# Letting five down-projection blocks be promised at once, with four written, in a kernel that plans its own TensorE order

## The chip, the core and the metric

The kernel runs on one core of one Trainium2 chip. The metric is the device time in microseconds (us) from launch to end, the median of several runs. A profile of one execution goes with it; its span, from the first to the last instruction, is a little shorter than the device time.

## The reference, cut to what matters

Two attention steps with 32 learned queries, then a gated feed-forward layer on each of the 4 x 12416 rows of 128 channels. Nearly all the work is in the last four lines.

```python
def mab(q, kv):                                  # attention without projections
    s = scale * (q @ kv.transpose(0, 2, 1)); s = s - s.max(-1, keepdims=True)
    a = np.exp(s); a /= a.sum(-1, keepdims=True) + 1e-09
    return a @ kv
h = mab(I, x)                                    # 32 rows per batch, from all of x
x = mab(x, h).reshape(B * S, D)                  # 49664 x 128
rms = np.sqrt(np.mean(x * x, axis=-1, keepdims=True) + 1e-06)
xn = x / rms * rms_g
g = xn @ w_gate; silu = g * (1.0 / (1.0 + np.exp(-g)))   # 128 -> 1536
val = xn @ w_val                                         # 128 -> 1536
return (silu * val @ w_out).astype(np.float32)           # 1536 -> 128
```

## The kernel before

The feed-forward part is cut into 100 *units* of up to 512 rows (25 per batch: 20 of 512 rows, 4 of 480, 1 of 256), and each unit into 12 *slots*, one per block of 128 hidden channels: 1200 slots. A slot makes a gate product and a value product on TensorE (PE), silu on ScalarE (ACT), and their product `t` on VectorE (DVE):

```python
def slot(j, products, steps, tanh):
    products(0)
    g = bank()
    nc.tensor.matmul(g[:, 0:T], sg[:, ts(j, P)], a[:, 0:T], start=True, stop=True)         # L682
    sl = silp.tile([P, 512], F32, name="silu")
    ...
        nc.scalar.activation(sl[:, 0:T], g[:, 0:T], AF.Silu)                               # L690
    products(1)
    v = bank()
    nc.tensor.matmul(v[:, 0:T], sv[:, ts(j, P)], a[:, 0:T], start=True, stop=True)         # L693
    t = v if kinds.get((b, u, j)) == "sums" else up.tile([P, 512], F32, name="u")
    ...
        nc.vector.tensor_tensor(out=t[:, 0:T], in0=sl[:, 0:T], in1=v[:, 0:T], op=ALU.mult) # L699
    steps()
    if (b, u, j) in kinds:
        soon(1, lambda: three(j, t))
    else:
        plain.append(lambda: project(wo[:, j, :], t[:, 0:T]))                              # L618, f32
```

Each block `t` then has to go through the down projection, `t` times 128 rows of `w_out`, added up in PSUM over the unit's 12 blocks. There are two ways. A *plain* block is one float32 product (`acc<-u,wo`). A *split* block is written as two float32r factors and a difference of them, and takes three float32r products (`u<-xn,xn`, a second one into `u`, `acc<-xn,more`) with weights that were split in the same manner. Splitting costs work on other engines; it has two forms, *sums* and *differences*:

```python
def three(j, t):
    assert kws.get("out", 0) < RING
    ...                                            # hi, lo, d: one of RING = 4 sets of buffers, in turn
    if kind == "sums":
        nc.scalar.activation(hi, v, AF.Copy, scale=(1.0 - 2.0 ** -13) * 2.0 ** -12)        # L664 ACT
        nc.vector.scalar_tensor_tensor(out=lo, in0=hi.bitcast(F32), scalar=-4096.0, in1=v, # L665 DVE
                                       op0=ALU.mult, op1=ALU.add)
    else:
        nc.scalar.activation(d, v, AF.Copy, scale=1.0 - 2.0 ** -13)                        # L668 ACT
        nc.gpsimd.tensor_tensor(out=lo, in0=v, in1=d.bitcast(F32), op=ALU.subtract)        # L669 POOL
    def rest():
        if kind != "sums":
            nc.scalar.activation(hi, d.bitcast(F32), AF.Copy, scale=2.0 ** -12)            # L673 ACT
        nc.gpsimd.tensor_tensor(out=d, in0=hi.bitcast(F32), in1=lo.bitcast(F32), op=ALU.subtract)  # L674 POOL
        kara.append(lambda: project3(j, hi, lo, d))
    soon(1, rest)

def project3(j, hi, lo, d):
    ...
    nc.tensor.matmul(ups[:, 0:T], weight_of(0, j), hi, start=st["k"] == nk, stop=False)    # L638
    nc.tensor.matmul(ups[:, 0:T], weight_of(1, j), lo, start=False, stop=not st["k"])      # L640
    if not st["k"]:                                # the unit's last split block
        o = st["o"] = outp.tile([P, 512], F32, name="o")
        nc.scalar.activation(o[:, 0:T], ups[:, 0:T], AF.Copy, scale=1.0 + 2.0 ** -12)      # L643 ACT
    project(weight_of(2, j), d)                                                            # L618
    kws["out"] -= 1
```

`soon(1, ...)` runs a step at the end of the next slot: a block whose `t` belongs to slot n is written to a set of ring buffers in slot n+1 (`three`), finished in slot n+2 (`rest`), and its products come later. A unit that has split blocks also needs one addition more at its end, on DVE (L626).

Which blocks are split, and when each product is issued, is decided before any instruction is recorded, by a *rehearsal*. It walks through the slots with a clock for each engine, fed with costs written in the kernel, and keeps the result in `kinds` (which blocks, which form) and `picks` (which products go ahead of the gate product and of the value product in each slot). Its parts that matter here:

```python
MADE = {"sums": ((-.16,), (0, .6, .49), (0, 0, 0, 1.25)), "differences": ((-.16,), (0, 0, .53, 1.25), (0, 0, .52, 1.25))}
LIMIT = (0, 0.8, 0.8, 2.6)

def fits(k, kind, behind):         # would any engine fall too far behind PE in the next 8 slots?
    ...
    before = list(ahead())
    load(k, *MADE[kind])
    if all(x <= max(most, y + 0.1) for now, old in zip(ahead(), before) for x, y, most in zip(now, old, LIMIT)):
        return True
    load(k, *MADE[kind], sign=-1)

def decide(b, k, u, j):
    n = b * NU * NJ + k
    if (j >= NK or b == 0 and (u < 2 or k < 26) or (b, u) == flat[-1] and j > 6 or split["out"] > RING - 1 or
            near(b, k, -3, 2)):
        return None                # a plain block
    ...
    return next((kind for kind in ("sums", "differences") if fits(n, kind, behind)), None)
```

In each slot of the rehearsal, `choose` issues products that are ready while more than about `RESERVE` blocks are queued, `fill` issues more where PE would wait for a PSUM bank, and a loop issues plain blocks whose `u` buffer is needed again (9 of them, `LAG + 4`). `RESERVE` is 6. Elsewhere in the slots stand the steps of the attention for the next batch and the normalisation ("seam") steps, among them one slow power operation on GpSimd (POOL, L521).

Of the kernel before, what the change touches and what calls it, by code (L numbers as in the profile page):

```python
# [17 lines left out]

P = 128
R = 4  # L20
LAG = 5


@with_exitstack
def kernel(
# [72 lines left out]
    NU = len(units)  # L98

    NK = NJ - 2  # L100
    RING, RESERVE = 4, 6

    def pool(name, bufs, **kw):
        return ctx.enter_context(tc.tile_pool(name=name, bufs=bufs, **kw))
# [8 lines left out]
    once = pool("once", 1)  # L113
    halves = pool("halves", 1)
    astk = pool("astk", 2)
    silp = pool("silp", 3)
    up = pool("up", LAG + 4)
    outp = pool("outp", 2)
    ps_gv = pool("ps_gv", 5, space=PSUM)
    ps_acc = pool("ps_acc", 2, space=PSUM)  # L120
# [77 lines left out]
    if wide:  # L198
        t = scp.tile([P, SCW], F32, name="sc")
# [365 lines left out]
    plain, kara, waiting = [], [], []  # L565
# [175 lines left out]
    one = weight[1, 0]  # L741
# [39 lines left out]
    turn_a, square, turn_z, scale, root, apply, turn_b, split = seam(0, 0)  # L781
# [39 lines left out]
    def load(k, *costs, sign=1):  # L821
        for i, one in enumerate(costs):
            for e, us in enumerate(one):
                loads[k + i][e] += sign * us
# [72 lines left out]
    for k, (b, s) in enumerate(order):  # L897
# [5 lines left out]
        for late_by, one in enumerate(following):  # L903
            for i, step in enumerate(seam(*one)):
                j = ((14, 17, 18, 21, 22, 23, 29, 31) if k else (32, 33, 34, 35, 36, 36, 39, 41))[i]
                n, j = divmod(j, NJ)
# [4 lines left out]
    flat = [(b, u) for b in range(B) for u in range(NU)]  # L911
# [11 lines left out]
    def near(b, k, first, last):  # L923
        return any(e + first <= k < e + last for e in plans[b][1])

    def given(b, k, u, j):
        return plans[b][0].get(k, []) + seams.get((b, u, j), [])

    LIMIT = (0, 0.8, 0.8, 2.6)
    kinds, picks = {}, {}  # L930

    def rehearse():

        at = dict.fromkeys(ENGINES, 0.0)
        free, open_banks = [0.0] * 5, {}
        queues, uses, later, left = {"plain": [], "three": []}, [0], [], {}
        split = {"out": 0, "u3": 0.0, "all": 0}

        def run(e, us, *after):
            at[e] = max([at[e]] + [one + 0.04 for one in after]) + us  # L940
            return at[e] + TAIL[e]

        def bank():
            return free.index(min(free))

        def soon(k, step):
            later.append([k, step])
# [7 lines left out]
        def issue(kind, to):  # L955
            to.append(kind)
            t, unit, w = queues[kind].pop(0)[:3]
            split["all"] -= 1
            st = left[unit]
            if kind == "plain":  # L960
                end = run("PE", 0.858 * w, t)
            else:
                if st["three"] == 0:
                    run("PE", 0, split["u3"])
                end = run("PE", 0.697 * w, t)
                split["out"] -= 1
                st["three"] += 1
                st["open"] -= 1
            st["left"] -= 1
            st["end"] = end  # L970
            if not st["left"] and st["all"]:
                close(unit, w)

        def close(unit, w):
            st = left[unit]
            if st["three"]:
                split["u3"] = run("ACT", 0.47 * w, st["end"])

            def finish():
                run("DVE", 0.6 * w, st["end"], split["u3"])  # L980
                soon(1, lambda: run("DVE", 0.63 * w))

            soon(1, finish)

        def choose(to, most):
            done = 0
            while done < most:
                now = at["PE"] + 0.05
                if has("three", now):
                    issue("three", to)  # L990
                elif has("plain", now):
                    issue("plain", to)
                else:
                    break
                done += 1
            return done

        def fill(to, until):
            while until > at["PE"] + 0.25:
                now = at["PE"] + 0.05  # L1000
                kind = next((kind for kind in ("three", "plain") if has(kind, now)), None)
                if kind is None:
                    break
                issue(kind, to)
# [20 lines left out]
        def fits(k, kind, behind):  # L1025

            def ahead():
                now = list(behind)
                for i in range(k, k + 8):
                    now = [max(0.0, x + one - loads[i][0]) for x, one in zip(now, loads[i])]  # L1030
                    yield list(now)

            before = list(ahead())
            load(k, *MADE[kind])
            if all(x <= max(most, y + 0.1) for now, old in zip(ahead(), before) for x, y, most in zip(now, old, LIMIT)):
                return True
            load(k, *MADE[kind], sign=-1)

        def decide(b, k, u, j):
            n = b * NU * NJ + k  # L1040
            if (j >= NK or b == 0 and (u < 2 or k < 26) or (b, u) == flat[-1] and j > 6 or split["out"] > RING - 1 or
                    near(b, k, -3, 2)):
                return None
            s = at["PE"]
            behind = [0.0] + [max(0.0, at[e] - s - off) for e, off in (("DVE", 1.2), ("ACT", 0.45), ("POOL", 1.45))]
            return next((kind for kind in ("sums", "differences") if fits(n, kind, behind)), None)

        def slot(b, k, u, j, tanh):
            w = per2[units[u][0]] * m / 512.0
            st = left.setdefault((b, u), dict(left=NJ, three=0, open=0, all=False, slots=0, end=0.0))  # L1050
            kind = decide(b, k, u, j)
            first, second = picks[b, k] = [], []
            gi = bank()
            fill(first, free[gi])
            g = run("PE", 0.2325 * w, free[gi])
            silu = run("ACT", 0.5 * w, g)
            if tanh:
                silu = run("DVE", 0.6 * w, silu)
            free[gi] = silu
            least = 1 if near(b, k, 0, 4) or (b, u) == flat[-1] else RESERVE + 2 * near(b, k, -2, 0)  # L1060
            choose(second, min(2, max(0, split["all"] - least + 1)))
            if kind != "sums":
                uses[0] += 1
                while queues["plain"] and queues["plain"][0][3] <= uses[0] - (LAG + 4):
                    issue("plain", second)
            vi = bank()
            fill(second, free[vi])
            v = run("PE", 0.2325 * w, free[vi])
            t = run("DVE", 0.6 * w, v, silu)
            free[vi] = 1e9 if kind == "sums" else t  # L1070
            for one in later:
                one[0] -= 1
            while any(not one[0] for one in later):
                one = next(one for one in later if not one[0])
                later.remove(one)
                one[1]()
            names = [step.__name__ for step, _ in given(b, k, u, j)]
            for name in names:
                if name in ("exp1_of", "exp2") and k in plans[b][1]:
                    run("ACT", 1.28)  # L1080
                do(name)
            if near(b, k, 2, 3):
                run("ACT", 1.28)
            if kind:
                kinds[b, u, j] = kind
                split["out"] += 1
                st["open"] += 1

                def three():
                    hi = run("ACT", (0.49 if kind == "sums" else 0.53) * w, t)  # L1090
                    if kind == "sums":
                        lo = free[vi] = run("DVE", 0.6 * w, hi)
                    else:
                        lo = run("POOL", 1.25 * w, hi)

                    def rest():
                        h = hi if kind == "sums" else run("ACT", 0.52 * w, hi)
                        d = run("POOL", 1.25 * w, lo, h)
                        queues["three"].append((d + 0.05, (b, u), w))

                    soon(1, rest)

                soon(1, three)
            else:
                queues["plain"].append((t + 0.05, (b, u), w, uses[0]))
            split["all"] += 1
            st["slots"] += 1
            if st["slots"] == NJ:
                st["all"] = True
                if not st["left"]:  # L1110
                    close((b, u), w)

        for b in range(B):
            for k, (u, j) in slots(b):
                slot(b, k, u, j, (b, k) in by_tanh)
        return at

    rehearsed = rehearse()

    for b in range(B):  # L1120
# [59 lines left out]
```

## Time and profile before

| | |
|---|---|
| device time, median of 3 runs | 1646.5 us (1646.23 to 1646.5) |
| span of the profiled execution | 1644.2 us |
| TensorE (PE) busy | 1620.6 us, 99% |
| VectorE (DVE) busy | 1431.0 us, 87% |
| ScalarE (ACT) busy | 1156.8 us, 70% |
| GpSimd (POOL) busy | 1007.2 us, 61% |
| granted TensorE clock | 0.999 |
| split blocks | 603 of 1200 |

How to read it: a matmul's recorded duration overlaps that of the next one, so the distance between the starts of two neighbours tells what one costs PE, and not its duration. The same holds, less strongly, for DVE, ACT and POOL, whose records also overlap a little when one instruction follows another directly. In the groups, "out<-in" names the tiles; a float32 matmul has two records, a float32r matmul has one. The ring buffers of the split blocks carry the name `xn`, the split weights `xn` or `more`.

### The profile page before, as it was taken

The numbers are of one execution on the slowest core, as the hardware profiler recorded it, in microseconds if no ns is written. First come the engines' busy times: TensorE is split into PE (matmuls) and PEld (weight loads), VectorE is DVE, ScalarE is ACT, GpSimd is POOL, SyncE is SP. The second block draws the span as 40 slices with busy tenths as digits, with TensorE's granted clock in tenths as the row PEclk, the third lists the DMA queues.
The fourth block names the chain that finished last, engine by engine and source line by source line (L and its number), as shares of the span: only waits on it lengthen the run. The fifth ranks groups of instructions, "written<-read, shape, count | busy, mean of one in ns | idle before, by whom it ended". The sixth has DMA issues, their size and how long they took to land.

```text
span 1644.2 us, 24663 instructions
## 1 busy us (share of the span) xinstructions
PE 1620.6 (99%) x6983; PEld 1070.2 (65%) x6983; DVE 1431.0 (87%) x2469; ACT 1156.8 (70%) x2104; POOL 1007.2 (61%) x804
## 2 busy tenths in 40 slices
PE   8899999999999999999999999999999999999998
PEld 6545666656676666665667666666567676666676
DVE  4878987899899998889889999789989999999997
ACT  4566777767776777676777676766677777777775
POOL 1246763766467755476567575466747767767764
PEclk9999999999999999999999999999999999999999
DMA  6455434443453241624435324253221112212221
GB/s 259 90 71 84 82 65 84 102 95 59 68 87 60 42 90 29 135 70 84 70 58 82 60 39 88 55 124 74 49 38 35 32 31 39 39 28 38 39 37 25
DMA packets 389176, 112.47 MB, mean 68 GB/s; under 512 B 365072, under 2 KB 369712, under 8 KB 386480
## 3 DMA queue, kind: packets, MB, share of 16 engines
q1 hardware_dynamic: 388304, 110.82, 34.3%
q8 instruction: 55, 0.90, 0.2%
q14 instruction: 81, 0.66, 0.1%
q10 hardware_dynamic: 736, 0.08, 0.0%
HBM read 53.95 MB, written 27.00 MB: 49 GB/s over the span
## 4 chain that ended last, share of the span: by engine, by line
PE 89%; DVE 2%; ACT 2%; issue 1%; POOL 1%; SPq 1%; DMA 1%; DVEq 0%; POOLq 0%; ACTq 0%
PE acc L618 35%; PE gv L682 17%; PE gv L693 15%; PE u L640 8%; PE u L638 8%; PE gv L327 3%; PE gv L504 1%; PE gv L383 1%; ACT sc L444 1%; POOL rs L521 0%; DVE u L699 0%; SPq L147 0%; PE gv L458 0%; DVE xn L665 0%; ACT silu L690 0%
## 5 line engine op out<-in xcount | busy, mean ns | idle before, releaser
L674 POOL TENSOR_TENSOR xn<-xn,xn 128x512 fp32r<-128x512 f32 (+2 forms) x603 | 750.1, 1255 | 451.1 <-DVE xn L665 271.4
L690 ACT ACTIVATE silu<-gv 128x512 f32<-128x512 f32 (+2 forms) x1186 | 689.7, 586 | 375.6 <-PE gv L682 351.5
L693 PE MATMUL gv<-a,sv 128*128 128x512 f32 (+2 forms) x1188 | 680.2, 573 | 0.5 <-ACT silu L690 0.2
L618 PE MATMUL acc<-u,wo 128*128 128x512 f32 (+2 forms) x1194 | 591.6, 580 | 0.0
L682 PE MATMUL gv<-a,sg 128*128 128x512 f32 (+2 forms) x1188 | 486.2, 409 | 3.9 <-ACT silu L690 2.4
L699 DVE TENSOR_TENSOR u<-silu,gv 128x512 f32<-128x512 f32 (+2 forms) x650 | 423.3, 659 | 59.0 <-PE gv L693 41.7
L699 DVE TENSOR_TENSOR gv<-silu,gv 128x512 f32<-128x512 f32 (+2 forms) x536 | 359.8, 673 | 86.8 <-PE gv L693 66.7
L665 DVE SCALAR_TENSOR_TENSOR xn<-xn,gv 128x512 fp32r<-128x512 f32 (+2 forms) x537 | 354.4, 660 | 9.8 <-ACT xn L664 5.5
L682 PEld LDWEIGHTS gv<-a,sg 128*128 128x128 f32 x1188 | 224.5, 189 | 207.4 <-ACT silu L690 45.0
L664 ACT ACTIVATE xn<-gv 128x512 fp32r<-128x512 f32 (+2 forms) x537 | 314.6, 586 | 52.2 <-DVE gv L699 44.1
L693 PEld LDWEIGHTS gv<-a,sv 128*128 128x128 f32 x1188 | 224.4, 189 | 157.4 <-issue 77.1
L618 PEld LDWEIGHTS acc<-u,wo 128*128 128x128 f32 x1194 | 224.0, 189 | 55.3 <-issue 12.0
L618 PE MATMUL acc<-xn,more 128*128 128x512 f32 (+2 forms) x603 | 235.1, 390 | 2.6 <-POOL xn L674 2.6
L638 PE MATMUL u<-xn,xn 128*128 128x512 f32 (+2 forms) x603 | 233.2, 387 | 0.0
L640 PE MATMUL u<-xn,xn 128*128 128x512 f32 (+2 forms) x356 | 137.7, 387 | 0.0
L618 PEld LDWEIGHTS acc<-xn,more 128*128 128x128 f32 x603 | 113.3, 188 | 29.9 <-POOL xn L674 6.3
L638 PEld LDWEIGHTS u<-xn,xn 128*128 128x128 f32 x603 | 113.4, 188 | 24.1 <-issue 4.2
L521 POOL TENSOR_TENSOR rs<-ms,mhalf 128x16 f32<-128x16 f32 (+2 forms) x28 | 75.9, 2710 | 68.8 <-DVE ms L516 68.0
L669 POOL TENSOR_TENSOR xn<-u,xn 128x512 fp32r<-128x512 f32 (+1 forms) x66 | 85.1, 1289 | 19.3 <-ACT xn L668 19.1
L640 PE MATMUL u<-xn,more 128*128 128x512 f32 (+2 forms) x247 | 95.9, 388 | 0.0
L640 PEld LDWEIGHTS u<-xn,xn 128*128 128x128 f32 x356 | 66.9, 188 | 15.2 <-issue 0.2
L629 DVE STREAM_TRANSPOSE o<-o 128x512 f32<-128x512 f32 (+2 forms) x92 | 63.0, 685 | 0.0
(151 smaller groups left out, 1009.1 us busy)
## 6 DMA issues: line engine op xcount, KB each, us to landing
out_dram<-o SPq DMA_DIRECT2D x320, 64.0 KB, 2.0
xT<-in_x_dram SPq DMA_DIRECT2D x60, 256.0 KB, 4.7
xn<-in_x_dram SPq DMA_DIRECT2D x60, 256.0 KB, 5.1
a<-hi SPq DMA_DIRECT2D x156, 64.0 KB, 2.0
a<-lo SPq DMA_DIRECT2D x156, 64.0 KB, 2.0
xn<-in_x_dram SPq DMA_DIRECT2D x5, 1024.0 KB, 9.9
xn<-w SPq DMA_DIRECT2D x18, 256.0 KB, 3.2
out_dram<-o SPq DMA_DIRECT2D x64, 60.0 KB, 2.0
```

The source lines that it names most:

```text
L521: nc.gpsimd.tensor_tensor(out=rs, in0=st["ms"], in1=mhalf[rows, 0:n], op=ALU.pow)
L618: nc.tensor.matmul(acc[:, 0:T], lhsT, rhs, start=st["left"] == NJ, stop=st["left"] == 1)
L638: nc.tensor.matmul(ups[:, 0:T], weight_of(0, j), hi, start=st["k"] == nk, stop=False)
L640: nc.tensor.matmul(ups[:, 0:T], weight_of(1, j), lo, start=False, stop=not st["k"])
L664: nc.scalar.activation(hi, v, AF.Copy, scale=(1.0 - 2.0 ** -13) * 2.0 ** -12)
L665: nc.vector.scalar_tensor_tensor(out=lo, in0=hi.bitcast(F32), scalar=-4096.0, in1=v, op0=ALU.mult, op1=ALU.add)
L669: nc.gpsimd.tensor_tensor(out=lo, in0=v, in1=d.bitcast(F32), op=ALU.subtract)
L674: nc.gpsimd.tensor_tensor(out=d, in0=hi.bitcast(F32), in1=lo.bitcast(F32), op=ALU.subtract)
L682: nc.tensor.matmul(g[:, 0:T], sg[:, ts(j, P)], a[:, 0:T], start=True, stop=True)
L690: nc.scalar.activation(sl[:, 0:T], g[:, 0:T], AF.Silu)
L693: nc.tensor.matmul(v[:, 0:T], sv[:, ts(j, P)], a[:, 0:T], start=True, stop=True)
L699: nc.vector.tensor_tensor(out=t[:, 0:T], in0=sl[:, 0:T], in1=v[:, 0:T], op=ALU.mult)
```

## The change

It changes the rehearsal alone; buffers, arithmetic and the engines' instructions for one block stay as they are. It is meant to let more blocks take the three-product way, and to keep TensorE from meeting a factor that isn't ready.

- Ring sets are now counted from when `three` writes them (`split["made"]`) and not from when the block is decided. A block may be decided while four others are outstanding (`> RING` in place of `> RING - 1`), so five are decided at most and four written. Where all four sets are written and a further `three` is due in this slot, one split block is issued first.
- `RESERVE` goes from 6 to 7: one more block stays outstanding before `choose` issues any.
- `fits` lets an engine's backlog that is already over its limit grow by 0.25 us, where it was 0.1.
- silu in the rehearsal waits for its buffer (three of them). `LAG` is gone; `HELD` is the same nine `u` buffers as before.

```diff
-    RING, RESERVE = 4, 6
+    RING, RESERVE, HELD, SILU = 4, 7, 9, 3
...
-    silp = pool("silp", 3)
-    up = pool("up", LAG + 4)
+    silp = pool("silp", SILU)
+    up = pool("up", HELD)
...
+        taken = [0.0] * SILU
-        split = {"out": 0, "u3": 0.0, "all": 0}
+        split = {"out": 0, "u3": 0.0, "all": 0, "made": 0}
...
                 split["out"] -= 1
+                split["made"] -= 1
...
-            if all(x <= max(most, y + 0.1) for now, old in zip(ahead(), before) for x, y, most in zip(now, old, LIMIT)):
+            if all(x <= max(most, y + 0.25) for now, old in zip(ahead(), before) for x, y, most in zip(now, old, LIMIT)):
...
-            if (j >= NK or b == 0 and (u < 2 or k < 26) or (b, u) == flat[-1] and j > 6 or split["out"] > RING - 1 or
+            if (j >= NK or b == 0 and (u < 2 or k < 26) or (b, u) == flat[-1] and j > 6 or split["out"] > RING or
...
-            silu = run("ACT", 0.5 * w, g)
+            silu = run("ACT", 0.5 * w, g, taken[-SILU])
...
-                while queues["plain"] and queues["plain"][0][3] <= uses[0] - (LAG + 4):
+                while queues["plain"] and queues["plain"][0][3] <= uses[0] - HELD:
                     issue("plain", second)
+            while split["made"] == RING and any(one[0] == 1 and one[1].__name__ == "three" for one in later):
+                issue("three", second)
...
             t = run("DVE", 0.6 * w, v, silu)
+            taken.append(t)
...
                 def three():
+                    split["made"] += 1
```

More of the change, by code (lines that the diff above doesn't have):

```diff
@@ L20 @@
 R = 4
-LAG = 5
 @with_exitstack
```

## The prediction

> **What bounds the kernel now.** I read the first page from the top: busy shares, slices, groups. TensorE stands at 99% in every slice, at full clock.
>
> ```profile
> PE 1620.6 (99%) x6983; PEld 1070.2 (65%) x6983; DVE 1431.0 (87%) x2469; ACT 1156.8 (70%) x2104; POOL 1007.2 (61%) x804
> PE   8899999999999999999999999999999999999998
> PEclk9999999999999999999999999999999999999999
> ```
>
> A busy share of 99% proves little, since the records of matmuls overlap. So the second view is TensorE's timeline, where only the starts are read. First a stretch with split blocks, then one with plain blocks alone.
>
> ```profile
> 600.76 0.40 PE L682 MATMUL gv<-a,sg 128*128 128x512 f32 x1
> 600.99 0.39 PE L638 MATMUL u<-xn,xn 128*128 128x512 f32 x1
> 601.23 0.40 PE L640 MATMUL u<-xn,more 128*128 128x512 f32 x1
> 601.46 0.40 PE L618 MATMUL acc<-xn,more 128*128 128x512 f32 x1
> 601.69 0.40 PE L693 MATMUL gv<-a,sv 128*128 128x512 f32 x1
> ```
>
> ```profile
> 250.79 0.40 PE L682 MATMUL gv<-a,sg 128*128 128x512 f32 x1
> 251.02 1.88 PE L618 MATMUL acc<-u,wo 128*128 128x512 f32 x4
> 252.34 0.80 PE L693 MATMUL gv<-a,sv 128*128 128x512 f32 x1
> 252.98 0.40 PE L682 MATMUL gv<-a,sg 128*128 128x512 f32 x1
> ```
>
> Starts are 0.233 us apart, so a gate or value product costs 0.233 and a split block three of them, 601.69 - 600.99 = 0.70 us. From 250.79 to 252.98 there is one gate, one value and two plain blocks (four records): 2.19 - 2 x 0.233 = 1.72, or 0.86 us for a plain block. A split block saves TensorE 0.16 us at 512 columns.
>
> Third, is there slack in TensorE's stream? Adding these costs over the whole timeline from 100 us on, with about 1.0 us for the four matmuls of a score step and 0.87 for a normalisation square, leaves some 26 us unexplained in 1540. So the stream is closed to under 2%, and the end is the sum of TensorE's work. The open gaps are few. The largest kind by far in the last batch is this one, in the timeline of all engines:
>
> ```profile
> 1355.45 2.90 POOL L521 TENSOR_TENSOR rs<-ms,mhalf 128x16 f32<-128x16 f32 x1 [1.25 <-DVE ms L516]
> ...
> 1358.32 1.28 POOL L674 TENSOR_TENSOR xn<-xn,xn 128x512 fp32r<-128x512 f32 x1
> ...
> 1358.55 0.40 PE L640 MATMUL u<-xn,more 128*128 128x512 f32 x1
> ...
> 1359.65 0.50 PE L618 MATMUL acc<-xn,more 128*128 128x512 f32 x1 [0.71 <-POOL xn L674]
> ```
>
> The power operation holds GpSimd for 2.90 us, the factor d is finished late, and the third product of the block waits (0.71 us idle, about 0.87 by the starts). It recurs near 1420 and 1481, and with 0.45 us near 1542: 2.6 us in all.
>
> **What the Trainium skill says.** "Perfetto Trace Analysis", section "Identifying the Most-Contended Engine", says that matmul busy time misjudges the distance to the limit because matmuls are pipelined. This trace agrees: records of 0.39 to 0.40 us whose starts are 0.233 apart. "TensorE: Matmul & The Clock Gate", section "Back-to-back issue gap", gives N/2.4 + 2.5 ns for an isolated gap, 216 ns for 512 columns, and a shorter one for a sustained stream of bf16; the trace shows 233 ns here and I use that. "Perfetto Trace Analysis", section "Optimizing Scalar/DVE Operations", says that half of an instruction's access overhead overlaps with the next one; the trace agrees, as DVE records of 0.68 us follow each other at 0.60 us, so an 87% busy DVE is less full than it looks. "GPSIMD Engine Reference", section 3.1, gives about 2.6 cycles an element for a two-input tensor operation, an estimate of 1.11 us for 512 columns from that page at its 1.2 GHz; the trace has 1.29 us, and 1.24 between starts.
>
> **The change, part by part.** The instruction list of the built program shows what the new rehearsal decides. These are the rows of the page that its counts are held against:
>
> ```profile
> L674 POOL TENSOR_TENSOR xn<-xn,xn 128x512 fp32r<-128x512 f32 (+2 forms) x603 | 750.1, 1255 | 451.1 <-DVE xn L665 271.4
> L618 PE MATMUL acc<-u,wo 128*128 128x512 f32 (+2 forms) x1194 | 591.6, 580 | 0.0
> L665 DVE SCALAR_TENSOR_TENSOR xn<-xn,gv 128x512 fp32r<-128x512 f32 (+2 forms) x537 | 354.4, 660 | 9.8 <-ACT xn L664 5.5
> L669 POOL TENSOR_TENSOR xn<-u,xn 128x512 fp32r<-128x512 f32 (+1 forms) x66 | 85.1, 1289 | 19.3 <-ACT xn L668 19.1
> ```
>
> Before: 603 split blocks, 537 by sums and 66 by differences, and 597 plain ones (1194 records). After: 706 split, 568 by sums (+31) and 138 by differences (+72), and 494 plain. Of the 103 that change side, 79 have 512 columns, 17 have 480 and 7 have 256: 79 + 17 x 0.9375 + 7 x 0.5 = 98.4 full blocks.
>
> - TensorE: 98.4 x (0.86 - 0.70) = 15.7 us less, all on the path that sets the end.
> - DVE: 31 remainders at 0.60, and 8 units more that need a closing addition (92 units had one, now 100): 39 x 0.60 = 23 us more. With spacing in place of durations DVE's share goes from about 1431 x 0.60/0.68 = 1263 us to 1286 us of some 1630, 79%. Beside other work.
> - ACT: 31 x 0.49 + 72 x (0.54 + 0.52) + 8 x 0.48 = 95 us more, to about 77% by its records. Beside other work.
> - GpSimd: 31 x 1.25 + 72 x 2.50 = 219 us more, 1226 us in all, 75%. Beside other work while it keeps ahead of TensorE's order.
> - What is moved: `RESERVE` 7 lengthens the way from a block to its products. Counted in the two instruction lists in slots (the half is for products ahead of the value product): sums from 5.4 to 5.7 on average, differences from 5.8 to 6.5; products only 4.5 slots or less behind fall from 124 blocks to 35. At 1.2 to 1.3 us a slot that is 0.4 us more for sums and 0.9 us for differences. It should close most of the gap shown above: I count 1.5 us of its 2.6.
> - The ring: at most five are decided, four written, and the list keeps to it, so no engine overwrites a set that TensorE still needs. A forced product comes no sooner than 3.5 slots behind, in 7 blocks, as before. Counting and silu's buffer cost nothing by themselves.
> - New waits: I allow 2 us, by the rivals below.
>
> Sum: 1646.5 - 15.7 - 1.5 + 2 = 1631.3; I say 1631.5.
>
> **The rivals.** First, GpSimd becomes the wait. A block by differences takes it twice. A cluster such as sums, differences, differences, sums, sums is 7 operations of 1.25, 8.8 us, in five slots that last TensorE 5 x 1.17 = 5.8 us: GpSimd falls 3 us behind. A difference block's own chain is 0.54 + 1.25 + 0.52 + 1.25, about 3.6 us and some wakeups from the slot after its own; its products come 6.5 slots, about 8 us, behind. It fits by a margin of one to two microseconds, and less where the power operation of 2.90 us falls into the cluster. If half of the 72 new difference blocks met a wait of 0.25 us, 9 us would be lost and the time would be 1641. Against it: GpSimd was idle 39% of the time, and the longer distance was given to just these blocks.
>
> Second, DVE becomes the bound in the dense units. The first unit of a new batch has eight split blocks where it had seven, beside normalisation steps; summing spacing for spacing, DVE's work there is 6% more than TensorE's, where it was 3% less. DVE makes `t`, and a late `t` keeps a PSUM bank from the next gate product. That would cost about 1 us in each of three such units, 3 us in all, and 1634. In the other units, but for the very first, the sum stays at or under 0.96 of TensorE's.
>
> Third, the larger allowance lets backlog grow where the old rule stopped it, and ACT's silu, queued behind splitting work, holds up gate and value. In the page, ACT's largest idle time is waiting for gate products, 351.5 us, which speaks against it. At worst I give it a few us.
>
> Fourth, TensorE time is not what ends the run, so that nothing comes of it. The starts above speak against it.
>
> **Range and chances.** The gain of 15.7 us is counted and its price per block measured, so it is good to about 1 us. The waits are the open part: between 4 us better and 7 us worse than I allow. So 1628 to 1638 us should hold it 8 times in 10, with the upper side longer. 2% would be below 1613.6 or above 1679.4 us; the first would need twice the saving, the second 48 us of new waits. Chances: faster by over 2% 0.01, within 2% 0.98, slower by over 2% 0.01.
>
> **What would show it right or wrong.** The group `acc<-u,wo` should have 988 records and `acc<-xn,more` 706, with starts still 0.233 and 0.86 apart; PE still 98 to 99% busy; GpSimd near 1226 us busy. The waits of TensorE on L674 should not exceed some 4 us in total, and the pattern near 1359 should shrink. I am wrong if TensorE's idle time ahead of products of split blocks, or ahead of gate products for DVE, adds up to more than some 8 us, or if plain and split blocks don't cost what their starts say.

## The result, and the profile after

The changed kernel takes 1637.5 us (median of 4 runs, 1637.2 to 1638.9) beside 1646.4 for the kernel before: a ratio of 0.9949, 95% interval 0.9932 to 0.9966. The gain is 8.8 us. That is inside the range of 1628 to 1638 us, half a microsecond from its upper end: 6 us more than the predicted 1631.5.

The first page of the changed kernel shows the decisions as counted (line numbers are one lower from here on, as `LAG` is gone):

```profile
PE 1608.4 (98%) x7086; PEld 1084.5 (66%) x7086; DVE 1444.4 (88%) x2506; ACT 1246.0 (76%) x2285; POOL 1217.5 (74%) x979
PE   8899999999999999999999999999999999999998
...
L673 POOL TENSOR_TENSOR xn<-xn,xn 128x512 fp32r<-128x512 f32 (+2 forms) x706 | 872.0, 1255 | 305.9 <-DVE xn L664 169.5
...
L617 PE MATMUL acc<-u,wo 128*128 128x512 f32 (+2 forms) x988 | 489.5, 580 | 0.0
...
L664 DVE SCALAR_TENSOR_TENSOR xn<-xn,gv 128x512 fp32r<-128x512 f32 (+2 forms) x568 | 373.1, 657 | 9.0 <-ACT xn L663 6.2
...
L668 POOL TENSOR_TENSOR xn<-u,xn 128x512 fp32r<-128x512 f32 (+1 forms) x138 | 177.3, 1285 | 5.4 <-ACT xn L667 5.4
```

706 split blocks, 988 records of plain ones, GpSimd at 1217.5 us. So TensorE's work fell as planned; what is left to find is where a good part of it went. The line view of the down projection (the two kinds of product that write `acc`: plain ones, and the third product of a split block) says how long TensorE and its weight loads sat idle before it. Columns: total us, times. First the kernel before, then the changed one:

```profile
its engine sat idle before it (us, times) until:
  issue: 12.0, 51
  POOL xn L674: 8.9, 15
  DVE u L699: 0.6, 2
```

```profile
its engine sat idle before it (us, times) until:
  POOL xn L673: 16.2, 27
  issue: 9.9, 42
  DVE o L625: 4.1, 5
```

Two things are new here: the wait for the factor d (POOL) has nearly doubled, and there is one that the kernel before doesn't have at all, for L625. L625 is the addition at a unit's end, which reads the unit's accumulator bank. This view counts idle weight loads and idle matmuls both, so its numbers rank waits and don't add up to lost time.

For lost time I use the starts. For each matmul from 54 us on, where the first value product runs, I take the distance to the next start, less the usual distance (the lower quartile) of the same two neighbours, after the same predecessor, at the same width, over all the kernels of this study:

| TensorE, us | before | after |
|---|---|---|
| sum of the usual distances | 1520.9 | 1501.9 |
| more than usual, all pairs | 64.1 | 74.4 |
| of it: second to third product of a split block | 5.1 | 10.6 |
| gate to value product | 0.8 | 4.0 |
| third product to value product | 2.4 | 3.6 |
| first to second product | 0.8 | 1.8 |
| value product to an attention step | 4.1 | 1.6 |

Some 33 us of the second row, in both kernels alike, lie between the small matmuls of the attention and play no part here. The rows on split blocks and the one from gate to value product stay within about 1 us however the widths of the neighbours are grouped; the totals, and the pairs that end at a gate product or an attention step, move by some 4 us.

So 19.0 us of work went and 10.3 us of waiting came. At 98.4 blocks the price of a block (0.172 us, from the kernel with no split blocks below) makes 16.9 of the 19.0; the other 2.1 sit in rare pairs of neighbours, where this method can't tell waiting from work. Either way 8 to 10 us of new waits stand where the prediction had 0.5 on balance. Over half of them are ahead of the third product of a split block.

The rise between gate and value product shows on the pages, too. What TensorE waits for there is silu (before, then after):

```profile
L693 PE MATMUL gv<-a,sv 128*128 128x512 f32 (+2 forms) x1188 | 680.2, 573 | 0.5 <-ACT silu L690 0.2
L692 PE MATMUL gv<-a,sv 128*128 128x512 f32 (+2 forms) x1188 | 634.9, 534 | 2.4 <-ACT silu L689 2.2
```

### The profile page after: what moved, and what is told of

It is laid out like the page before. It is cut to its first block, busy times and chain, and to the rows that moved or that the text cites. A ratio compares the mean times of both kernels' runs of the same rounds, so it can differ in the third digit from the quotient of the medians.

```text
span 1635.7 us, 25441 instructions
## 1 busy us (share of the span) xinstructions
PE 1608.4 (98%) x7086; PEld 1084.5 (66%) x7086; DVE 1444.4 (88%) x2506; ACT 1246.0 (76%) x2285; POOL 1217.5 (74%) x979
## 4 chain that ended last, share of the span: by engine, by line
PE 85%; DVE 4%; issue 3%; ACT 2%; POOL 2%; DMA 1%; SPq 0%; DVEq 0%; ACTq 0%; POOLq 0%
PE acc L617 31%; PE gv L681 16%; PE gv L692 15%; PE u L637 9%; PE u L639 9%; PE gv L326 3%; PE gv L503 1%; DVE gv L698 1%; PE gv L382 1%; ACT silu L689 1%; DVE u L698 1%; POOL rs L520 1%; POOL xn L673 1%; DVE xn L664 1%; PE gv L457 0%
## 5 line engine op out<-in xcount | busy, mean ns | idle before, releaser
L673 POOL TENSOR_TENSOR xn<-xn,xn 128x512 fp32r<-128x512 f32 (+2 forms) x706 | 872.0, 1255 | 305.9 <-DVE xn L664 169.5
L692 PE MATMUL gv<-a,sv 128*128 128x512 f32 (+2 forms) x1188 | 634.9, 534 | 2.4 <-ACT silu L689 2.2
L617 PE MATMUL acc<-u,wo 128*128 128x512 f32 (+2 forms) x988 | 489.5, 580 | 0.0
L698 DVE TENSOR_TENSOR u<-silu,gv 128x512 f32<-128x512 f32 (+1 forms) x619 | 407.3, 664 | 53.9 <-PE gv L692 33.3
L617 PE MATMUL acc<-xn,more 128*128 128x512 f32 (+2 forms) x706 | 275.1, 390 | 6.1 <-POOL xn L673 2.9
L637 PE MATMUL u<-xn,xn 128*128 128x512 f32 (+2 forms) x706 | 272.9, 387 | 0.9 <-ACT o L642 0.7
L617 PEld LDWEIGHTS acc<-u,wo 128*128 128x128 f32 x988 | 184.6, 188 | 46.3 <-issue 9.4
L668 POOL TENSOR_TENSOR xn<-u,xn 128x512 fp32r<-128x512 f32 (+1 forms) x138 | 177.3, 1285 | 5.4 <-ACT xn L667 5.4
L639 PE MATMUL u<-xn,xn 128*128 128x512 f32 (+2 forms) x413 | 159.8, 387 | 0.1
L637 PEld LDWEIGHTS u<-xn,xn 128*128 128x128 f32 x706 | 132.7, 188 | 31.2 <-issue 4.6
L667 ACT ACTIVATE xn<-u 128x512 fp32r<-128x512 f32 (+1 forms) x138 | 87.0, 630 | 30.0 <-DVE u L698 23.1
L639 PEld LDWEIGHTS u<-xn,xn 128*128 128x128 f32 x413 | 77.5, 188 | 17.5 <-POOL xn L668 0.5
```

The source lines that it names most:

```text
L617: nc.tensor.matmul(acc[:, 0:T], lhsT, rhs, start=st["left"] == NJ, stop=st["left"] == 1)
```

## The experiments

Theories: (1) a split block really saves TensorE about 0.17 us, and new waits for late factors take half of it; (2) a split block is worth only some 0.09 us anywhere; (3) the loss sits in a few fixed places and GpSimd has no part in it; and, formed after the first four runs, (4) plain blocks that are kept waiting hold an accumulator bank, and the next unit but one waits for its read-out.

### The limit of four decided blocks put back

```diff
-split["out"] > RING or
+split["out"] > RING - 1 or
```

> The changed kernel with the old limit on decided blocks (four instead of five). 646 split blocks, 40.4 full-width blocks more than the kernel before, where the change has 98.4 more. Theory 1 (each split block really saves TensorE 0.17 us, and the loss is new waits for late factors and banks that grow with the density): at 0.17 us it would be 6.9 us under the kernel before; with few new waits, 1639 to 1641 us. Theory 2 (a split block is worth only about 0.09 us everywhere, as the change's 8.9 us over 98.4 blocks says): 1642.8 us.

Measured: 1641.7 us (1639.7 to 1643.5, 6 runs), ratio 0.997 (0.9958 to 0.9983). That lies between the two theories and its executions spread over 4 us (the last section says more), so it decides little.

### The allowance of 0.1 us put back

```diff
-y + 0.25
+y + 0.1
```

> The changed kernel with the old allowance of 0.1 us. 674 split blocks (590 by sums, 84 by differences), 66.9 full-width blocks more than before. Theory 1: the 54 difference blocks that are missing are those that meet late factors; 11.5 us saved less about 2 us of waits, 1636 to 1638 us, thus as fast as the change with a third less blocks. Theory 2 (0.09 us a block): 1640.3 us.

Measured: 1644.3 us (1643.0 to 1645.8, 20 runs), ratio 0.9989 (0.9983 to 0.9996). All theories missed: 66.9 full-width blocks more than before brought 2 us. TensorE's timeline of this kernel suggested a reason:

```profile
406.41 1.02 PE L617 MATMUL acc<-u,wo 128*128 128x512 f32 x2
...
407.70 0.38 PE L637 MATMUL u<-xn,xn 128*128 128x480 f32 x1
407.92 0.38 PE L639 MATMUL u<-xn,xn 128*128 128x480 f32 x1
409.72 0.45 PE L617 MATMUL acc<-xn,more 128*128 128x480 f32 x1 [1.42 <-DVE o L625]
```

The widths tell the units apart: the plain block at 406.41 belongs to a unit of 512 columns, the split block at 407.70 to a unit of 480. There are two accumulator banks, and the instruction list gives the two products their tiles: the plain one is the last of the unit two earlier (`acc_3917`), the split one is the first of the unit that takes over its bank (`acc_4267`).

```
1125 L617 Matmult acc_3917<-u_4083,wo_109 128x512
1130 L617 Matmult acc_4267<-xn4_939,more_135 128x480 [waits DVE_49,Pool_49]
```

Between them DVE has to run L625, which the kernel records one slot later, behind DVE's other work. So the next matmul starts 1.80 us after the second product, where 0.22 us is usual: 1.6 us are lost. This is what theory 4 says. In the changed kernel the same happens, here at the start of the second batch (TensorE, then DVE):

```profile
472.24 0.97 PE L617 MATMUL acc<-u,wo 128*128 128x480 f32 x2
...
474.41 0.39 PE L637 MATMUL u<-xn,xn 128*128 128x512 f32 x1
474.65 0.40 PE L639 MATMUL u<-xn,xn 128*128 128x512 f32 x1
475.93 0.47 PE L617 MATMUL acc<-xn,more 128*128 128x512 f32 x1 [0.89 <-DVE o L625]
```

```profile
473.94 0.69 DVE L698 TENSOR_TENSOR gv<-silu,gv 128x512 f32<-128x512 f32 x1
474.54 0.68 DVE L664 SCALAR_TENSOR_TENSOR xn<-xn,gv 128x512 fp32r<-128x512 f32 x1
475.13 0.65 DVE L625 TENSOR_TENSOR o<-acc,o 128x480 f32<-128x480 f32 x1
```

The bank's last product starts at 472.24; L625 runs at 475.13, without a gap on DVE before it, and only then may the third product go. It repeats at 871.76 and 1267.35.

From the instruction lists one can count, for each kernel, the units whose first product comes 2 slots or less after the last product of the unit that held their bank: none before (the nearest is 5), 14 in the changed kernel, 15 with the old allowance, 3 with the old limit on decided blocks, none with `RESERVE` 6. (The expectations below say 13 and 14; the last unit of the program has to be added.)

### RESERVE 6 put back

```diff
-RING, RESERVE, HELD, SILU = 4, 7, 9, 3
+RING, RESERVE, HELD, SILU = 4, 6, 9, 3
```

> The changed kernel with RESERVE 6 as before. 718 split blocks, 110.3 full-width blocks more than before, but products follow their blocks more closely. Theory 1: the waits for factors grow; slower than the change by 1 to 5 us, 1639 to 1642 us, with over 3 us more of wait ahead of the third product. Theory 2: 1636.4 us, a little faster than the change, as only the count matters.

Measured: 1636.9 us (1636.1 to 1637.1, 4 runs), ratio 0.9942 (0.9927 to 0.9957): the same as the change within the intervals. The wait ahead of third products fell (10.6 to 7.6 us by the starts) where theory 1 had it grow by 3, and no wait for L625 is left:

```profile
its engine sat idle before it (us, times) until:
  POOL xn L673: 15.8, 37
  issue: 10.7, 46
  DVE u L698: 0.6, 2
```

Theory 2's 1636.4 fits the number; its price per block falls further down. So `RESERVE` 7, meant to give factors more time, brings the bank's wait here. It needs the other edits for that: alone, in the kernel before, it brings none (below).

### The third product reads hi in place of d, in the changed kernel and in the one before

```diff
-            project(weight_of(2, j), d)
+            project(weight_of(2, j), hi)
```

GpSimd still makes d; the result lacks it.

> The changed kernel in which the third product of a split block reads the factor hi in place of d. GpSimd still makes d, but TensorE never waits for it there; what is left out is the difference d in the result. Theory 1: TensorE lost 10.6 us by the starts ahead of third products in the change, about 3 of which is for an accumulator bank; without d's wait 5 to 7 us of that go, 1631 to 1633 us. Theory 3 (the loss sits in a few fixed places that wait for banks and silu, and GpSimd is innocent): at most 2 us faster, 1635.5 us or more.

> The kernel before with the third product reading hi in place of d, so that the difference d is left out of the result. Its starts show 3.3 us of waits of over 0.6 us at four places ahead of third products: 1642 to 1644 us. The change gained 3.2 us from the same edit; if the loss of the change lies mainly in waits for d, the gain here must be clearly smaller, under 2 us.

Measured: 1634.3 us (1634.0 to 1636.5, 4 runs) for the changed kernel, 3.2 us less; 1641.5 us (1640.8 to 1642.6, 7 runs) for the one before, 5.0 us less. With d's wait gone, the waits of the changed kernel that remain show the other cause bare, in 13 places where the list has 14 such units:

```profile
its engine sat idle before it (us, times) until:
  DVE o L625: 9.8, 13
  issue: 9.4, 41
```

By the starts, d costs 3.8 us ahead of third products in the kernel before (5.1 to 1.3) and 5.2 in the changed one (10.6 to 5.4). So by the starts the wait for d grew by 1.4 us and the rest, nearly all of it the bank, by 4.1. By the times d costs no more in the changed kernel (3.2 us) than in the one before (5.0). Part of what d's wait takes there would be lost to the bank without it: waits for L625 go from 4.1 us in 5 places to 9.8 in 13 when d is not read. Theory 1 in its narrow form, that the loss is GpSimd's lateness, falls: the kernel before gains more from the same edit. Theory 3 falls as well, as 3.2 us is more than it allowed.

### Old blocks first

In the last two slots of a unit, plain blocks of an earlier unit go ahead of split ones:

```diff
+        def late(unit):
+            (b, u), j = where[0]
+            return unit[0] * NU + unit[1] < b * NU + u and j >= 10
...
-                if has("three", now):
+                if has("three", now) and not (has("plain", now) and late(queues["plain"][0][1])):
...
+            where[0] = (b, u), j
```

> The changed kernel, whose rehearsal issues plain blocks of an earlier unit first in the last two slots of a unit. 710 split blocks (686.8 full-width ones, the change has 682.9); no unit's first product comes within 5 slots of the last product of the unit that held its accumulator bank, where the change has 13 units at 2 slots. Theory 4 (new: long-waiting plain blocks keep an accumulator bank, and the next unit's first product waits for its read-out): the waits of 1.05 us at three places and of 0.28 us at five or more go, 4 to 6 us, 1632 to 1634 us. Theory 1 in its old form (only factors from GpSimd are late): no change, 1636.5 to 1638 us.

> The same order of products with the old allowance of 0.1 us. 673 split blocks, 650.3 full-width ones, as many as the kernel with the old allowance alone, which took 1644.3 us and has 14 units at 1 or 2 slots. Theory 4: that kernel lost about 10 us ahead of third products to the bank; here 1634 to 1637 us. Theory 2 or 1: 1642 us or more.

> The same order of products with RESERVE 6. 718 split blocks, 694.8 full-width ones. The kernel with RESERVE 6 alone (1636.9 us) has no unit that follows closely on its bank, so theory 4 gives the new order nothing here: 1635.5 to 1638 us. If the order helps for another reason, it is faster here as well, by 3 us or more.

Measured: 1635.0 us (1633.8 to 1636.4, 4 runs) on top of the change, 2.5 us less, and none of its executions reaches the 1637.2 to 1638.9 of the change; 1634.5 us (1634.4 to 1635.2, 4 runs) with the old allowance, where the same kernel without the new order took 1644.3: 9.8 us less with 0.2% fewer full-width blocks; 1638.1 us (1637.2 to 1638.4, 4 runs) with `RESERVE` 6, 1.2 us more than without the order, the same within the intervals of the two ratios. Theory 4 told all three to about 1 us: much where the bank was short, some where less, nothing where it wasn't. (On top of the change one unit comes 4 slots after its bank's last product, not 5; it doesn't bear on this.) The line view of the kernel with the old allowance and the new order has no L625 in it:

```profile
its engine sat idle before it (us, times) until:
  issue: 11.3, 48
  POOL xn L673: 4.3, 11
  DVE u L698: 0.6, 2
```

At the place of 407.92 above, the plain block of the unit two earlier is gone: it was issued four slots sooner, ahead of these lines. A split block of the unit between stands there (512 columns), and no gap is left ahead of the new unit's third product (480 columns):

```profile
406.48 0.39 PE L637 MATMUL u<-xn,xn 128*128 128x512 f32 x1
406.70 0.39 PE L639 MATMUL u<-xn,more 128*128 128x512 f32 x1
406.93 0.40 PE L617 MATMUL acc<-xn,more 128*128 128x512 f32 x1
...
408.11 0.38 PE L639 MATMUL u<-xn,xn 128*128 128x480 f32 x1
408.33 0.38 PE L617 MATMUL acc<-xn,more 128*128 128x480 f32 x1
```

On top of the whole change the order gains less than its 4 us of bank waits: ahead of third products 4.0 us go (10.6 to 6.6), but plain block to value takes 2.4 more, and value to gate up to 2.3 more, depending on how the widths are grouped. With 686.8 full-width blocks the kernel is no faster than with 650.3: at this density the added blocks only pay for their waits.

### A multiplication in place of the power operation

```diff
-in1=mhalf[rows, 0:n], op=ALU.pow)
+in1=mhalf[rows, 0:n], op=ALU.mult)
```

This leaves the normalisation out of the result.

> The changed kernel with a multiplication in place of the power operation on GpSimd, so that the normalisation is left out; the time of that operation is expected to fall from 2.9 us to well under 1. If the power operation is what makes the factor d late, the waits ahead of third products that follow it (0.3 to 0.5 us of idle at seven places, 1.1 at one by the starts) go, 3 to 4 us, 1633.5 to 1634.5 us. If GpSimd's splitting work is late by itself: at most 1 us, 1636.5 us or more.

Measured: 1633.4 us (1632.7 to 1634.2, 4 runs), 4.1 us less than the change. The operation fell from a median of 2.90 us to 0.22, and by the line view the waits for d from 16.2 us in 27 cases to 6.0 in 7, while L625 stays as it was:

```profile
its engine sat idle before it (us, times) until:
  issue: 9.9, 42
  POOL xn L673: 6.0, 7
  DVE o L625: 4.1, 5
```

By the starts 4.4 of the 5.2 us that d costs go (10.6 to 6.2 ahead of third products). So d is late, for the most part, where the power operation runs ahead of it on GpSimd. That operation stood there before the change, too; no run tells whether as much GpSimd time freed at another place would help as well. One such place in the changed kernel:

```profile
1349.30 2.90 POOL L520 TENSOR_TENSOR rs<-ms,mhalf 128x16 f32<-128x16 f32 x1 [0.66 <-DVE ms L515]
1352.16 1.29 POOL L673 TENSOR_TENSOR xn<-xn,xn 128x512 fp32r<-128x512 f32 x1
1352.82 0.39 PE L639 MATMUL u<-xn,more 128*128 128x512 f32 x1
...
1353.51 0.50 PE L617 MATMUL acc<-xn,more 128*128 128x512 f32 x1 [0.30 <-POOL xn L673]
```

### No split blocks at all

```diff
-        return next((kind for kind in ("sums", "differences") if fits(n, kind, behind)), None)
+        return None
```

> The kernel before with no split block at all: all 1200 blocks take the one float32 product. Measures the price of a block over a large count: 584.5 full-width blocks change side. If a split block saves TensorE 0.16 to 0.17 us, as the starts say, 1646.3 + 94 to 101 = 1740 to 1747 us, a little less if the waits that splitting brings go too (1735 and up). If a split block is worth only the 0.09 us that the change got: 1699 us.

Measured: 1725.1 us (1723.9 to 1726.4, 2 runs), ratio to the kernel before 1.048 (1.0461 to 1.0499). Both expectations missed: it is under the 1735 us and up that went with a price of 0.16 to 0.17 us, and far over 1699. 78.7 us over 584.5 blocks are 0.135 each. The starts close the sum: the usual distances add up to 1621.3 us, 100.4 more than before, which is 0.172 a block, and what exceeds them is 43.4 us, 20.7 less. 100.4 - 20.7 = 79.7. So the price of a block is 0.172 (0.8605 for a plain one, 3 x 0.2295 for a split one), and even in the kernel before a fifth of it went into waits. Theory 2 is wrong as a price. What a block brings on balance did fall, from 0.135 over the first 584 to 0.09 over the 98 of the change, but that is the order of products as much as their number: with old blocks first and the old allowance 65.8 blocks more than before brought 11.9 us, 0.18 each, and the next 36.5 nothing.

### RESERVE 7 alone

```diff
-    RING, RESERVE = 4, 6
+    RING, RESERVE = 4, 7
```

> The kernel before with RESERVE 7 alone. 608 split blocks, 2.6 full-width ones more, and products half a slot later; no unit within 5 slots of its bank's last product. The prediction held that the later products close 1.5 of the 2.6 us of waits for d: with 0.4 us for the blocks, 1644 to 1645 us. If the waits for d don't depend on the distance: 1646 us.

Measured: 1646.3 us (1644.5 to 1646.8, 13 runs), ratio 0.9999 (0.9991 to 1.0007). Nothing. Ahead of third products it gains most of what was hoped (5.1 to 3.9 us by the starts), but gate to value goes from 0.8 to 2.7, or more with another grouping of widths. The wait moves. Nor are split products half a slot later, as the expectation has it: in the built program they come 5.4 slots (sums) and 5.6 (differences) after their block on average, where it was 5.4 and 5.8. The plain ones come later, 9.5 slots where it was 7.5.

### A version that beats both

Old blocks first, the old allowance, and a rehearsal that takes the power operation for longer than it is, to keep splitting work away from it:

```diff
-"root": (0, 0, 0, 2.9)
+"root": (0, 0, 0, 3.6)
```

> The kernel with old blocks first and the old allowance (1634.5 us), whose rehearsal takes the power operation for 3.6 us in place of 2.9, so that it puts less splitting work beside it: 670 split blocks, 647.4 full-width ones, 2.8 fewer. If the waits that are left come from that operation, 1633 to 1634.5 us; if not, the missing blocks cost 0.5 us: 1635 us. An attempt at a faster version.

Measured: 1633.5 us (1631.6 to 1633.8, 4 runs), ratio 0.9921 (0.9907 to 0.9934): the fastest that gives the whole result, 4 us under the change with 35.5 full-width blocks fewer. Against the 1634.5 us without the longer power operation the difference is within the scatter; waits for d went on falling:

```profile
its engine sat idle before it (us, times) until:
  issue: 11.3, 48
  POOL xn L673: 1.7, 7
  DVE u L698: 0.6, 2
```

## Why the prediction was right, and where it was not

- **The decisions and TensorE's work.** Right in count (706, 988, +31, +72), but for the closing additions: 98 units have one (L625), 6 more than before and not 8, which moves nothing. The price was sized a little low: 0.16 from starts in hundredths, 0.172 when measured, so 16.9 us in place of 15.7.
- **The bound.** Right: TensorE stays at 98%, and the sum over its starts gives the time in every run. (The slices show 99% but for the first two and the last.) The "some 26 us unexplained" were about right: it is what the 64.1 us above leave, to a few us, without the 33 us inside the attention and the first 100 us. But they were taken as small, and not read: the kernel with no split blocks shows that splitting had already brought some 20 us of them, so that more splitting could be expected to bring more.
- **RESERVE 7 closes 1.5 us.** Wrong in effect and in mechanism. Alone it gains nothing, and it isn't what lengthens the way of split blocks: their 5.7 and 6.5 slots came with the other edits (5.6 and 6.2 with `RESERVE` 6 put back, 5.4 and 5.8 with the old allowance put back, 5.4 and 5.6 with `RESERVE` 7 alone). What it makes older is plain blocks: `choose` takes split blocks first, and a block by sums asks for no `u` buffer, so little pushes a plain block out. In the built programs plain products come at most 12 slots after their block before the change, 14 with `RESERVE` 7 alone and up to 16 after the change. That is a unit and a third, so they hold a bank that the next unit but one needs.
- **New waits, 2 us.** The step that failed, by size: with the 1.5 us above, 0.5 us on balance was forecast, and 8 to 10 came. By the starts about 4 us of them are the bank, 1.4 the factor d, 3.2 value products after gate products, and the remainder is spread. That the bank comes before d is shown by experiment; for the value products the trace names silu, and no run took their cause apart.
- **Its own signs.** The starts, the counts, GpSimd's 1217.5 us and the shrunken pattern (0.71 us of idle near 1359 before, 0.30 at 1353.51 now) came as told. But the waits on L673 are 16.2 us by the line view, where 4 were allowed (8.9 stood there before), and ahead of second and third products of split blocks the starts show 12.4 us more than usual (5.9 before), over the 8 that were to mean "wrong". By these signs the forecast of few new waits failed.
- **First rival, GpSimd.** Partly. The waits for d exist, but they stand mostly behind the power operation, and they grew by only 1.4 us. Clusters of difference blocks did no visible harm, and no visible good: with old blocks first, 135 difference blocks gave 1635.0 us and 89 gave 1634.5.
- **Second rival, DVE in a batch's first unit.** The places and the size were right (three units, about 1 us each: 475.93, 871.76, 1267.35), the mechanism wasn't. Not a late `t` and a bank for the gate product, but a late read-out L625 and the accumulator bank. That the places agree is in part luck.
- **Third and fourth rival.** Gate to value went from 0.8 to 4.0 us, which is "a few us" as the third had it at worst, and the page names silu, as it had it; that ACT's splitting work ahead of silu is the cause stays open. The fourth fell.
- **The ring and silu's buffer.** Right to give them nothing. With the line that has silu wait for its buffer taken out, or the one that forces a product, the rehearsal decides the same, block for block; the forced product never occurs.

The sum missed by 6 us, since the price was low by 1.2 us and the waits were low by 7.5. The range held because its upper side was long, and by luck: the median lies 0.5 us inside it, and one of the four executions (1638.9 us) outside.

## What to carry to other kernels

Before giving a scheduler more work to place, list every buffer that a waiting item holds, the accumulator it will write included: a queue that always prefers one kind can let the other grow old and keep what the next tile needs. A count of slots between the last use of a bank and its next first use, taken from the built program, told for every kernel here whether TensorE would wait for that bank; it says nothing of the waits for d and for silu. And price a change at the margin: a block was worth 0.135 us over the first 584 and 0.09 over the 98 of the change, and the kernel with 35 blocks fewer and no bank waits was the faster one.

## What the runs showed of the hardware

The granted TensorE clock isn't the same from run to run of one kernel, and with the limit of four decided blocks the time went with it: 1639.7 and 1640.4 us at 1.000, 1641.6 to 1642.2 at 0.998 and 1643.5 at 0.997. With the old allowance this shows less: 1643.0 to 1644.8 us at 0.999, 1643.8 to 1644.8 at 0.998 and 1645.8 at 0.997. The power operation on a tile of 128 x 16 takes GpSimd 2.90 us, over twice as long as one of its 128 x 512 subtractions (1.29); a multiplication of the same tile takes 0.22.
